# First loads in another order, keys and values of the second batch at later ticks, means of v in two column groups of TensorE

## The chip, the cores and the metric

The kernel runs on one core of one Trainium2 chip. The engines are TensorE (PE in the profile, its weight loads PEld), VectorE (DVE), ScalarE (ACT), GpSimd (POOL) and SyncE (SP), which here only issues loads and stores. The metric is the device time of one execution in microseconds; lower is better.

## The reference

Three layers follow each other: an attention with a window, a feed-forward layer with a softmax-like gate and a normalization, and a second feed-forward layer with ELU.

```python
# q, k, v: 2 batches, 8 heads, 768 positions, 64 channels
k_sum = k.reshape(B, H, nb, 32, D).max(axis=3)
v_sum = v.reshape(B, H, nb, 32, D).mean(axis=3)
scores_l = scale * q @ k.T            # kept where abs(i - j) < 16
scores_s = scale * q @ k_sum.T + log(32)
a = softmax(concat(scores_l, scores_s))
x = a @ concat(v, v_sum)              # 1536 tokens x 512
h = x @ w_in                          # 512 x 1024
solu = h * softmax(h)
ln = (solu - mean) / sqrt(var + 1e-6) * g_ln
x2 = ln @ w_out                       # 1024 x 512
h2 = x2 @ w_in2                       # 512 x 2048
out = elu(h2) @ w_out2                # 2048 x 512
```

The matrices w_in, w_out, w_in2 and w_out2 arrive as 64-bit floats (the `words` of the launch are their halves).

## The kernel before, in words

**Attention.** A unit n is 64 positions of one batch, all eight heads; there are 24, twelve per batch. `attn_s(n)` copies the 96 keys of its window beside the 24 block maxima into one of three buffers `kw` on POOL, multiplies on PE (`s_ps`, with `q_bd[n]`, a load of 256 KB), adds the mask and takes the maximum on DVE, takes the exponential on ACT, the reciprocal on DVE, and scales the four head pairs on POOL (`sm`). `attn_p(n)` transposes on PE (`p_ps`) and copies on ACT (`pT`). `attn_x(n)` multiplies with the values (`x_ps`; `vw`, three buffers, with 96 rows of v loaded by `load_v` and 24 rows of block means copied from `vsum` on POOL), and splits the result into a hi part (ACT) and a lo part (DVE), `xT`. Each value product writes 64 of the 128 output partitions: the even head of a pair the lower half, the odd head the upper.

**Sums over blocks.** `load_k(b)` loads the keys of a batch, four loads of 400 KB; `sum_k(b)` takes the block maxima with four reductions on DVE. `sum_v(b)` loads v in six tiles of 256 KB into the buffer `y[1]` (`rows[1]`) and forms the means with six matmuls of 512 columns with the matrix `avg`, which moves along so that the 24 sums of all six tiles add up in rows 96 to 119 of one PSUM tile, `vs_ps`; one ACT copy takes them to `vsum`.

**Conversions.** `convert` loads 512 KB of 64-bit words into a part of `y[0]` or `y[1]` (named y_65 and y_66 in the program) and makes 32-bit floats of them: ACT (line 113), POOL (114), DVE (115, 116, 117), then the hi part on ACT (120) and the lo part on DVE (95). For w_in there are eight such chunks, six buffers in turn (`early`); the last three of them lie in `y[1]`, where the v tiles lie too. Eight chunks of w_out follow (line 119 on POOL multiplies with g_ln). `more()` does the next one.

**Feed-forward.** A token tile j is 128 tokens. `mm_in(j, n)` is one half of h, twelve matmuls of 512 columns (`h`); after the second half `ffn1_ln(j)` begins with the row maximum on DVE (line 233). `mm_out` and the second layer follow.

**Order.** SP issues its loads in the order in which the code stands (a manual schedule), and waits at each for its buffer. The order on the other engines comes from a scheduler that works on the whole program. First comes a start written out by hand, and then a loop over 24 ticks, of which each does one half of h and the steps of attention units t+6 (scores), t+4 (transposes) and t+3 (values).

Of the kernel before, what the change touches and what calls it, by code (L numbers as in the profile page):

```python
# [14 lines left out]
AF = mybir.ActivationFunctionType  # L15
# [4 lines left out]
B, H, S, D = 2, 8, 768, 64  # L20
BLOCK, WINDOW = 32, 16
NB = S // BLOCK
TQ = 64
NT = S // TQ
WIN = 96
KW = WIN + NB
# [23 lines left out]
def tile_kernel(ctx: ExitStack, tc: tile.TileContext, qd, kT, v, w_in, w_out, g_ln, w_in2, w_out2,  # L50
                ident_d, mask_d, avg_d, out):
    nc = tc.nc
# [7 lines left out]
    ident = com.tile([128, 128], F32, name="ident")  # L60
# [20 lines left out]
    gT = p_ln.tile([128, KF1], F32, name="gT")  # L81
# [5 lines left out]
    avg = p_at.tile([128, 128 + NB], F32, name="avg", bufs=1)  # L87
    nc.gpsimd.memset(negh, -0.5)

    def copy_pool(out_, in_):  # L90
        nc.gpsimd.tensor_scalar(out_, in_, 1.0, 0.0, op0=ALU.mult, op1=ALU.add)


    def lo_of(out_, x, hi):
        nc.vector.tensor_tensor(out_, x, hi.bitcast(F32), op=ALU.subtract)  # L95
# [38 lines left out]
    k_sb, q_bd, xT, live, ksum, vsum = {}, {}, {}, {}, {}, {}  # L134

    def load_k(b):
        k_sb[b] = p_k.tile([128, NP, S + 2 * PAD], F32, tag="k", name="k_sb", bufs=2)
        for p in range(NP):
            nc.sync.dma_start(k_sb[b][:, p, :], kT[b, p])

    def sum_k(b):
        ksum[b] = p_at.tile([128, NP, NB], F32, name="ksum") if b else kws[0][:, :, WIN:KW]
        for p in range(NP):
            nc.vector.tensor_reduce(
                ksum[b][:, p, :], k_sb[b][:, p, PAD:PAD + S].rearrange("d (n j) -> d n j", j=BLOCK),
                axis=AX.X, op=ALU.max)


    def sum_v(b):
        pst = psb.tile([128, DM], F32, tag="b", name="vs_ps")  # L150
        for i in range(S // 128):
            vt = rows[1][i]
            nc.sync.dma_start(vt, v[b, PAD + i * 128:PAD + (i + 1) * 128, :])
            c0 = NB - i * 4
            nc.tensor.matmul(pst, lhsT=avg[:, c0:c0 + 128], rhs=vt, start=i == 0, stop=i == S // 128 - 1)
        vsum[b] = p_at.tile([128, DM], F32, tag="vsum", name="vsum", bufs=1)
        nc.scalar.activation(vsum[b][WIN:KW, :], pst[WIN:KW, :], AF.Copy)

    def load_q(n):
        q_bd[n] = p_at.tile([128, NP, 2 * TQ], F32, tag="q", name="q_bd", bufs=4)  # L160
        nc.sync.dma_start(q_bd[n], qd[n])

    def load_v(n):
        b, t = divmod(n, NT)
        nc.sync.dma_start(vws[n % NBUF][0:WIN, :], v[b, t * TQ:t * TQ + WIN, :])

    def attn_s(n):
        b, t = divmod(n, NT)
        j, half = divmod(n, 2)
        kw = kws[n % NBUF]  # L170
        if n not in q_bd:
            load_q(n)
        if t < NBUF and n:
            copy_pool(kw[:, :, WIN:KW], ksum[b])
        copy_pool(kw[:, :, 0:WIN], k_sb[b][:, :, t * TQ:t * TQ + WIN])
        sps = psb.tile([128, NP, 128], F32, tag="b", name="s_ps")
        for p in range(NP):
            nc.tensor.matmul(sps[:, p, 0:KW], lhsT=q_bd[n][:, p, :], rhs=kw[:, p, :], start=True, stop=True)  # L178
        sm = p_at.tile([128, NP, KW], F32, tag="sm", name="sm", bufs=NBUF)
        st = p_at.tile([128, 4, NP], F32, tag="st", name="st", bufs=NBUF)  # L180
        nm, ss, ri = (st[:, i, :] for i in range(3))
        mi = 1 if t == 0 else (2 if t == NT - 1 else 0)
        for p in range(NP):
            nc.vector.tensor_tensor_reduce(sm[:, p, :], sps[:, p, 0:KW], mask[:, mi, :], -scale, 3.0e38,
                                           op0=ALU.add, op1=ALU.min, accum_out=nm[:, p:p + 1])
        for p in range(NP):
            nc.scalar.activation(sm[:, p, :], sm[:, p, :], AF.Exp, bias=nm[:, p:p + 1], scale=-1.0,
                                 accum_out=ss[:, p:p + 1])
        nc.vector.tensor_scalar(ri, ss, 1e-9, None, op0=ALU.add)
        nc.vector.reciprocal(ri, ri)  # L190
        for p in range(NP):
            nc.gpsimd.tensor_scalar(sm[:, p, :], sm[:, p, :], ri[:, p:p + 1], 1.0, op0=ALU.mult, op1=ALU.mult)  # L192
        live[n] = sm
    def attn_p(n):
        pps = psb.tile([128, NP, 128], F32, tag="b", name="p_ps")
        for p in range(NP):
            nc.tensor.transpose(pps[:KW, p, :], live[n][:, p, :], ident)
        pT = p_at.tile([128, NP, 128], F32, tag="pT", name="pT")
        nc.scalar.activation(pT[:KW], pps[:KW], AF.Copy)
        live[n] = pT  # L200

    def attn_x(n):
        b, t = divmod(n, NT)
        j, half = divmod(n, 2)
        if t < NBUF:
            copy_pool(vws[n % NBUF][WIN:KW, :], vsum[b][WIN:KW, :])
        pT, vw = live.pop(n), vws[n % NBUF]
        if not half:
            xT[j] = [p_at.tile([128, NP, 128], F32R, tag=f"x{i}", name="xT", bufs=3) for i in range(2)]
        xps = psb.tile([128, NP, 128], F32, tag="b", name="x_ps")[:, :, :TQ]  # L210
        for p in range(NP):
            for hh in range(2):
                ds = slice(hh * D, (hh + 1) * D)
                nc.tensor.matmul(xps[ds, p, :], lhsT=vw[:KW, p * 128 + hh * D:p * 128 + (hh + 1) * D],  # L214
                                 rhs=pT[:KW, p, hh * TQ:(hh + 1) * TQ], start=True, stop=True)
        xh, xl = (a[:, :, half * TQ:(half + 1) * TQ] for a in xT[j])
        nc.scalar.activation(xh, xps, AF.Copy)
        lo_of(xl, xps, xh)
# [58 lines left out]
    def load_w3():  # L277
        f = len(w3)
        if f < 2:
            t = p_k.tile([128, 2, KD, 128], F32R, name=f"w3_{f}")  # L280
        elif f < 14:
            if f in (2, 5):
                state["k"] = p_k.tile([128, 3, 2, KD, 128], F32R, name=f"w3_{f}", tag="k", bufs=2)
            elif f in (8, 11):
                state["k"] = p_w3.tile([128, 3, 2, KD, 128], F32R, name=f"w3_{f}", tag=f"lnT{f // 11}")
            t = state["k"][:, (f - 2) % 3]
        else:
            t = p_w3.tile([128, 2, KD, 128], F32R, name=f"w3_{f}")
        w3.append((t[:, 0], t[:, 1]))
        convert(bits(), w_in2[:, f * 128:(f + 1) * 128].bitcast(I32).rearrange("(k p) f -> p k f", p=128),  # L290
                t[:, 0], t[:, 1])
# [33 lines left out]
    def more(n=1):  # L325
        for _ in range(n):
            if conv:
                conv.pop(0)()

    def mm_in(j, n):  # L330
        for k in range(KD):
            ffn1_in(j, n, k)
        if n == 1:
            ffn1_ln(j)
# [10 lines left out]
    loads = tc.manual_schedule(engines={mybir.EngineType.SP})  # L345
    loads.__enter__()
    load_k(0)
    load_q(1)
    load_v(0)
    nc.sync.dma_start(mask, mask_d)  # L350
    sum_k(0)
    nc.sync.dma_start(ident, ident_d)
    load_q(0)
    more()
    nc.sync.dma_start(avg, avg_d)
    attn_s(0)
    more()
    attn_s(1)
    sum_v(0)
    more(2)  # L360
    attn_p(0)
    attn_p(1)
    attn_s(2)
    attn_x(0)
    load_v(1)
    attn_x(1)
    nc.sync.dma_start(gT, g_ln)
    attn_s(3)
    load_v(2)
    attn_p(2)  # L370
    attn_s(5)
    attn_x(2)
    more(3)
    attn_p(3)
    attn_s(4)
    load_v(3)
    more()

# [9 lines left out]
    NU = B * NT  # L390
    for t, (j, n) in enumerate(ticks):
        s_n, p_n, x_n = t + LEAD, t + LEAD - 2, t + LEAD - 3
        if t == 0:
            sum_v(1)
        elif t == 1:
            load_k(1)
        elif t == 3:
            sum_k(1)
        if x_n < NU and t:
            load_v(x_n)  # L400
        if s_n < NU:
            for u in (s_n + 1, s_n):
                if u < NU and u not in q_bd:
                    load_q(u)
            attn_s(s_n)
        mm_in(j, n)
        if p_n < NU:
            attn_p(p_n)
        for f, *args in after[t]:
            f(*args)  # L410
        if x_n < NU:
            attn_x(x_n)
        more(converts.get(t, 0))
        if t in (13, 15):
            load_w3()
        if x_n == NU - 1:
            p_at.release()
            p_w3 = ctx.enter_context(tc.tile_pool(name="p_w3", bufs=1, side="left", reuse_waits="tile"))
            lnT_last = [p_w3.tile([128, KF1, TB], F32R, tag=f"lnT{c}", name="lnT") for c in range(2)]
# [134 lines left out]
```

## Time and profile before

| | |
|---|---|
| median of 3 runs | 507.53 us (506.18 to 510.06) |
| profiled execution | 510.05 us, span 508.3 us |
| PE busy | 482.9 us, 95% of the span |
| DVE busy | 292.2 us, 57% |
| ACT busy | 269.9 us, 53% |
| POOL busy | 136.3 us, 27% |
| loaded from memory | 42.93 MB |

The span is the time from the first to the last instruction; the execution's own time is 1.75 us longer. The shares are averages over stages that differ: the attention and the conversions lie in the first 200 us, the second layer in the last 300. Times below are counted from the span's start.

### The profile page before, as it was taken

The page shows a single profiled execution, that of the slowest core. Times are in us where ns is not written, and L with a number is a line of the kernel's source. Part 1 is how long each engine was busy: PE and PEld are TensorE (multiplying, and loading weights), DVE is VectorE, ACT ScalarE, POOL GpSimd, SP SyncE. Part 2 cuts the span into 40 slices and gives each one's busy share as a digit, 9 for nine tenths or more (in the row PEclk, how much of TensorE's full clock was granted, in tenths as well). Part 3 has the DMA queues.
Part 4 walks back from the last instruction along what each step waited for, and adds up shares of the span by engine and source line. Part 5 has one row for each costly group of instructions (what it writes and reads, how often), then busy time and mean ns, then how long its engine had stood idle before and what let it go on. Part 6 is the DMA issues. An engine that isn't in the chain of part 4 may idle for free.

```text
span 508.3 us, 7746 instructions
## 1 busy us (share of the span) xinstructions
PE 482.9 (95%) x2808; PEld 425.3 (84%) x2808; DVE 292.2 (57%) x714; ACT 269.9 (53%) x634; POOL 136.3 (27%) x216
## 2 busy tenths in 40 slices
PE   0888999899999999999999999999999999999997
PEld 0564877688888898999889999999998999999895
DVE  2688899697557126899999982222542323232331
ACT  1674898685657235766777763424452424242441
POOL 1877579589323111322132600000000000000000
PEclk9989999999999999999999999999999999999999
DMA  8967662261301010556455500000030000000003
GB/s 289 334 216 278 204 217 92 77 212 59 114 17 33 17 41 1 166 171 202 142 190 165 166 0 2 1 1 0 1 124 1 0 1 0 1 0 1 1 1 125
DMA packets 24567, 46.58 MB, mean 92 GB/s; under 512 B 2256, under 2 KB 11088, under 8 KB 24528
## 3 DMA queue, kind: packets, MB, share of 16 engines
q1 hardware_dynamic: 24528, 46.08, 28.1%
q8 instruction: 22, 0.36, 0.3%
q14 instruction: 17, 0.14, 0.1%
HBM read 42.93 MB, written 3.15 MB: 91 GB/s over the span
## 4 chain that ended last, share of the span: by engine, by line
PE 72%; DVE 12%; DMA 8%; ACT 3%; issue 2%; SPq 1%; POOL 1%; ACTq 0%; DVEq 0%
PE h L98 11%; PE h L100 11%; PE h L99 11%; PE o_ps L100 9%; PE o_ps L98 9%; PE o_ps L99 9%; DMA y<-in_w_out 4%; PE s_ps L178 3%; DVE conv L116 3%; DMA q_bd<-in_qd 3%; PE y_ps L98 2%; PE y_ps L100 2%; DVE conv L117 2%; PE y_ps L99 2%; PE x_ps L214 2%
## 5 line engine op out<-in xcount | busy, mean ns | idle before, releaser
L449 DVE SCALAR_TENSOR_TENSOR m<-m,h 128x384 f32<-128x384 f32 x64 | 35.2, 551 | 100.6 <-ACT m L448 100.6
L98 PE MATMUL h<-y_hl,w 128*128 128x384 f32 x256 | 86.2, 337 | 0.0
L100 PE MATMUL h<-y_hl,w 128*128 128x384 f32 x256 | 86.2, 337 | 0.0
L99 PE MATMUL h<-y_hl,w 128*128 128x384 f32 x256 | 86.2, 337 | 0.0
L447 ACT ACTIVATE m<-h 128x384 f32<-128x384 f32 x64 | 31.2, 487 | 84.4 <-PE h L100 84.3
L98 PE MATMUL o_ps<-w,g_hl 128*128 128x512 f32 x192 | 75.5, 393 | 0.1
L99 PE MATMUL o_ps<-w,g_hl 128*128 128x512 f32 x192 | 75.3, 392 | 0.0
L100 PE MATMUL o_ps<-w,g_hl 128*128 128x512 f32 x192 | 74.0, 392 | 0.0
L114 POOL TENSOR_SCALAR conv<-conv 128x512 f32<-128x512 f32 x48 | 38.2, 798 | 70.8 <-ACT conv L113 69.6
L192 POOL TENSOR_SCALAR sm<-sm,st 128x120 f32<-128x120 f32 x96 | 47.9, 518 | 23.1 <-DVE st L190 20.7
L95 DVE TENSOR_TENSOR g_hl<-m,g_hl 128x384 fp32r<-128x384 f32 x64 | 37.1, 580 | 27.3 <-ACT g_hl L450 27.2
L450 ACT ACTIVATE g_hl<-m 128x384 fp32r<-128x384 f32 x64 | 33.5, 524 | 33.9 <-DVE m L449 33.9
L99 PEld LDWEIGHTS h<-y_hl,w 128*128 128x128 f32 x256 | 48.0, 188 | 1.6
L98 PEld LDWEIGHTS h<-y_hl,w 128*128 128x128 f32 x256 | 48.0, 187 | 1.6
L100 PEld LDWEIGHTS h<-y_hl,w 128*128 128x128 f32 x256 | 48.0, 187 | 0.1
L178 PE MATMUL s_ps<-kw,q_bd 128*128 128x120 f32 x192 | 29.6, 301 | 15.5 <-DMA q_bd<-in_qd 14.0
L113 ACT ACTIVATE conv<-y 128x512 f32<-128x512 f32 x40 | 27.2, 679 | 32.1 <-DMA y<-in_w_in 11.4
L98 PE MATMUL y_ps<-lnT,w_out 128*128 128x384 f32 x128 | 43.8, 342 | 0.0
L99 PE MATMUL y_ps<-lnT,w_out 128*128 128x384 f32 x128 | 43.1, 337 | 0.0
L100 PE MATMUL y_ps<-lnT,w_out 128*128 128x384 f32 x128 | 42.8, 337 | 0.0
L100 PEld LDWEIGHTS o_ps<-w,g_hl 128*128 128x128 f32 x192 | 36.0, 188 | 7.8
L98 PEld LDWEIGHTS o_ps<-w,g_hl 128*128 128x128 f32 x192 | 36.0, 188 | 7.0 <-ACT g_hl L450 0.5
(77 smaller groups left out, 924.6 us busy)
## 6 DMA issues: line engine op xcount, KB each, us to landing
y<-in_w_out SPq DMA_DIRECT2D x23, 512.0 KB, 3.8
y<-in_w_in SPq DMA_DIRECT2D x17, 512.0 KB, 5.5
q_bd<-in_qd SPq DMA_DIRECT2D x24, 256.0 KB, 4.9
vw<-in_v SPq DMA_DIRECT2D x24, 192.0 KB, 4.1
bits<-in_w_in SPq DMA_DIRECT2D x7, 512.0 KB, 3.7
k_sb<-in_kT SPq DMA_DIRECT2D x8, 400.0 KB, 5.7
y<-in_v SPq DMA_DIRECT2D x12, 256.0 KB, 4.4
out<-y SPq DMA_DIRECT2D x11, 256.0 KB, 2.3
```

What stands on the lines that cost most here:

```text
L95: nc.vector.tensor_tensor(out_, x, hi.bitcast(F32), op=ALU.subtract)
L98: nc.tensor.matmul(ps, lhsT=l[0][ls], rhs=r[0][rs], start=first, stop=False)
L99: nc.tensor.matmul(ps, lhsT=l[0][ls], rhs=r[1][rs], start=False, stop=False)
L100: nc.tensor.matmul(ps, lhsT=l[1][ls], rhs=r[0][rs], start=False, stop=last)
L113: nc.scalar.activation(x, high.bitcast(F32), AF.Abs)
L114: nc.gpsimd.tensor_scalar(x, x, F64_HUGE, F64_TINY, op0=ALU.min, op1=ALU.max)
L116: nc.vector.scalar_tensor_tensor(a, high, -0x40000000, a, op0=ALU.bitwise_and, op1=ALU.bitwise_or)
L178: nc.tensor.matmul(sps[:, p, 0:KW], lhsT=q_bd[n][:, p, :], rhs=kw[:, p, :], start=True, stop=True)
L192: nc.gpsimd.tensor_scalar(sm[:, p, :], sm[:, p, :], ri[:, p:p + 1], 1.0, op0=ALU.mult, op1=ALU.mult)
L447: nc.scalar.activation(m, h2, AF.Relu, scale=-1.0)
L449: nc.vector.scalar_tensor_tensor(m, m, -1.0, h2, op0=ALU.add, op1=ALU.max)
L450: nc.scalar.activation(gh, m, AF.Copy)
```

## The change

Three things change. The loads of the start come in another order: q of unit 0 and the mask directly behind the keys, then q of unit 1, `avg` and the v tiles, and the identity, the value windows and the chunks of w_in after them. `load_k(1)`, `sum_k(1)` and `sum_v(1)` stand at ticks 2, 5 and 7 in place of ticks 1, 3 and 0. And the means use matmuls with 64 output partitions: tiles 0 to 2 add up in the lower half of the PSUM tile, 3 to 5 in the upper, taken in the order 0, 3, 1, 4, 2, 5; two ACT copies bring them together.

```diff
     def sum_v(b):
         pst = psb.tile([128, DM], F32, tag="b", name="vs_ps")
-        for i in range(S // 128):
+        for i in (0, 3, 1, 4, 2, 5):
             vt = rows[1][i]
             nc.sync.dma_start(vt, v[b, PAD + i * 128:PAD + (i + 1) * 128, :])
-            c0 = NB - i * 4
-            nc.tensor.matmul(pst, lhsT=avg[:, c0:c0 + 128], rhs=vt, start=i == 0, stop=i == S // 128 - 1)
+            g, c0 = i // 3, KW - 32 - i * 4
+            nc.tensor.matmul(pst[g * 64:(g + 1) * 64, :], lhsT=avg[:, c0:c0 + 64], rhs=vt,
+                             start=i % 3 == 0, stop=i % 3 == 2)
         vsum[b] = p_at.tile([128, DM], F32, tag="vsum", name="vsum", bufs=1)
         nc.scalar.activation(vsum[b][WIN:KW, :], pst[WIN:KW, :], AF.Copy)
+        nc.scalar.activation(vsum[b][WIN:WIN + NB // 2, :], pst[32:32 + NB // 2, :], AF.Copy)
...
     load_k(0)
-    load_q(1)
-    load_v(0)
+    load_q(0)
     nc.sync.dma_start(mask, mask_d)
     sum_k(0)
-    nc.sync.dma_start(ident, ident_d)
-    load_q(0)
-    more()
+    attn_s(0)
+    load_q(1)
     nc.sync.dma_start(avg, avg_d)
-    attn_s(0)
-    more()
     attn_s(1)
     sum_v(0)
-    more(2)
+    nc.sync.dma_start(ident, ident_d)
+    load_v(0)
+    more()
+    load_v(1)
+    more()
     attn_p(0)
     attn_p(1)
...
-        if t == 0:
+        if t == 2:
+            load_k(1)
+        elif t == 5:
+            sum_k(1)
+        elif t == 7:
             sum_v(1)
-        elif t == 1:
-            load_k(1)
-        elif t == 3:
-            sum_k(1)
```

The rest of the start (units 2 to 5, the six further chunks, g_ln) is rearranged in the same way. The order on the engines shows it. In these rows k_sb, q_bd, vw, mask, ident and avg are the tiles named above, y_65 the buffers of chunks 0, 1, 2, 6 and 7 of w_in, and y_66 those of chunks 3 to 5 and of the v tiles. Line numbers of the new kernel are up to 9 higher.

SP, the first loads of the program, before:

```order
L139 DMA k_sb<-in_kT 128x800 x4
L161 DMA q_bd<-in_qd 128x512
L165 DMA vw_101<-in_v 96x512
L350 DMA mask<-in_mask 128x360
L352 DMA ident<-in_ident 128x128
L161 DMA q_bd<-in_qd 128x512
L107 DMA y_65<-in_w_in 128x1024
L355 DMA avg<-in_avg 128x152
L107 DMA y_65<-in_w_in 128x1024
L153 DMA y_66<-in_v 128x512 x6
```

SP, the same place, now:

```order
L139 DMA k_sb<-in_kT 128x800 x4
L164 DMA q_bd<-in_qd 128x512
L352 DMA mask<-in_mask 128x360
L164 DMA q_bd<-in_qd 128x512
L356 DMA avg<-in_avg 128x152
L154 DMA y_66<-in_v 128x512 x6
L359 DMA ident<-in_ident 128x128
L168 DMA vw_101<-in_v 96x512
L107 DMA y_65<-in_w_in 128x1024
L168 DMA vw_102<-in_v 96x512
```

The first q was unit 1's and the second unit 0's; now unit 0 is first. The six v tiles moved ahead of all chunks of w_in.

POOL, from the key copy of unit 3 (into kw_98) to the copies of the means into the value windows, before; sm is the scaling of the scores, conv a step of a conversion:

```order
L91 TENSOR_SCALAR kw_98<-k_sb 128x4x96
L114 TENSOR_SCALAR conv<-conv 128x512
L91 TENSOR_SCALAR kw_99<-k_sb 128x4x96
L114 TENSOR_SCALAR conv<-conv 128x512
L192 TENSOR_SCALAR sm<-sm,st 128x120 x8
L114 TENSOR_SCALAR conv<-conv 128x512
L91 TENSOR_SCALAR vw_101<-vsum 24x512
L91 TENSOR_SCALAR vw_102<-vsum 24x512
L91 TENSOR_SCALAR vw_103<-vsum 24x512
```

POOL, the same place, now:

```order
L91 TENSOR_SCALAR kw_98<-k_sb 128x4x96
L91 TENSOR_SCALAR kw_99<-k_sb 128x4x96
L195 TENSOR_SCALAR sm<-sm,st 128x120 x8
L91 TENSOR_SCALAR vw_101<-vsum 24x512
L91 TENSOR_SCALAR vw_102<-vsum 24x512
L91 TENSOR_SCALAR vw_103<-vsum 24x512
L114 TENSOR_SCALAR conv<-conv 128x512 x2
```

The three conversion steps that stood ahead of the copies of the means stand behind them.

PE, where the means of the second batch stood among the matmuls of the first token tile, before:

```order
L178 MATMUL s_ps<-kw_99,q_bd 128x120 x4
L155 MATMUL vs_ps<-y_66,avg 128x512 x2
L98 MATMUL h<-w_in_82,xT 128x512
L197 MATMUL p_ps<-ident,sm 120x128 x2
L99 MATMUL h<-w_in_83,xT 128x512
L100 MATMUL h<-w_in_82,xT 128x512
L197 MATMUL p_ps<-ident,sm 120x128
L155 MATMUL vs_ps<-y_66,avg 128x512 x2
```

PE, where they stand now, between the value product of unit 9 and the matmuls of the fifth token tile (t_ps are the transposes of the normalized rows):

```order
L256 MATMUL t_ps<-ident,ln 128x128 x8
L217 MATMUL x_ps<-pT,vw_101 64x64 x8
L156 MATMUL vs_ps<-y_66,avg 64x512 x6
L98 MATMUL h<-w_in_82,xT 128x512
L99 MATMUL h<-w_in_83,xT 128x512
L181 MATMUL s_ps<-kw_99,q_bd 128x120 x4
```

The six matmuls moved behind those of four token tiles, and follow each other without another between them.

## Rows read from the trace of the kernel before

**Rows 1.** Busy time by stretch: us, then each engine's busy us, clock, DMA share, GB/s:

```profile
0.00:16.25 16.25, 4.60 (x19) 4.12 (x20) 5.55 (x21) 4.16 (x12) 3.88 (x13) 1.00 0.91 310
16.25:25.00 8.75, 6.57 (x24) 3.13 (x23) 6.86 (x16) 5.60 (x15) 8.33 (x12) 1.00 0.99 310
25.00:28.80 3.80, 3.80 (x44) 3.49 (x43) 2.12 (x11) 2.23 (x11) 2.58 (x4) 0.55 1.02 393
28.80:64.80 36.00, 31.76 (x222) 22.62 (x221) 31.00 (x108) 24.42 (x79) 24.99 (x44) 1.00 0.65 209
64.80:120.00 55.20, 51.68 (x386) 41.94 (x385) 48.98 (x170) 45.11 (x137) 43.72 (x73) 1.00 0.47 151
120.00:508.00 388.00, 384.49 (x2125) 349.99 (x2123) 197.67 (x394) 188.40 (x386) 52.78 (x73) 1.00 0.18 55
```

**Rows 2.** Waits of PE, 10 to 60 us: us in total, times, longest:

```profile
PE s_ps L178 <- DMA q_bd<-in_qd: 14.0, 3, 11.6
```

**Rows 3.** Timeline of SP's queue: start us, us, what is issued:

```profile
33.00 8.69 SPq L153 DMA_DIRECT2D y<-in_v  x6
```

**Rows 4.** The chain of work that ended last, 0 to 60 us: start us, us:

```profile
5.19 6.32 DMA q_bd<-in_qd
...
17.52 6.82 DMA q_bd<-in_qd
```

**Rows 5.** Timeline of PE, several stretches: start us, us, what, count:

```profile
11.65 3.68 PE L178 MATMUL s_ps<-kw,q_bd 128*128 128x120 f32 x16 [11.65 <-DMA q_bd<-in_qd]
15.16 4.53 PE L155 MATMUL vs_ps<-y,avg 128*128 128x512 f32 x10
...
25.60 1.98 PE L214 MATMUL x_ps<-pT,vw 120*64 120x64 f32 x32
...
38.24 1.89 PE L155 MATMUL vs_ps<-y,avg 128*128 128x512 f32 x4
...
63.90 0.50 PE L98 MATMUL h<-w_in,xT 128*128 128x512 f32 x1
...
96.87 0.69 PE L214 MATMUL x_ps<-pT,vw 120*64 120x64 f32 x16
97.48 1.15 PE L178 MATMUL s_ps<-kw,q_bd 128*128 128x120 f32 x8
```

**Rows 6.** Groups of DVE, 0 to 120 us: count, busy us, mean ns of one:

```profile
L116 DVE SCALAR_TENSOR_TENSOR conv<-y,conv 128x512 int32<-128x512 int32 x16 | 13.3, 831 | 0.2
L117 DVE SCALAR_TENSOR_TENSOR conv<-y,conv 128x512 int32<-128x512 int32 x16 | 11.7, 729 | 0.1
L115 DVE TENSOR_SCALAR conv<-conv 128x512 int32<-128x512 int32 x16 | 8.3, 521 | 1.0 <-POOL conv L114 1.0
...
L95 DVE TENSOR_TENSOR w_in<-conv,w_in 128x512 fp32r<-128x512 f32 x8 | 5.6, 695 | 1.4 <-ACT w_in L120 1.3
```

**Rows 7.** Timeline of DVE, three places: start us, us, what:

```profile
8.82 0.95 DVE L144 TENSOR_REDUCE kw<-k_sb 128x24 f32<-128x768 f32 x1 [0.50 <-DMA k_sb<-in_kT]
...
16.25 0.42 DVE L115 TENSOR_SCALAR conv<-conv 128x512 int32<-128x512 int32 x1
...
64.81 1.21 DVE L233 TENSOR_REDUCE st<-h 128x1 f32<-128x1024 f32 x1
```

**Rows 8.** Timeline of POOL, two stretches: start us, us, what, count:

```profile
17.25 5.62 POOL L192 TENSOR_SCALAR sm<-sm,st 128x120 f32<-128x120 f32 x8
...
23.65 2.57 POOL L91 TENSOR_SCALAR vw<-vsum 24x512 f32<-24x512 f32 x3
...
56.03 2.77 POOL L192 TENSOR_SCALAR sm<-sm,st 128x120 f32<-128x120 f32 x8 [3.57 <-DVE st L190]
```

**Rows 9.** Timeline of ACT, 12 to 27 us:

```profile
12.85 0.67 ACT L113 ACTIVATE conv<-y 128x512 f32<-128x512 f32 x1 [10.85 <-DMA y<-in_w_in]
...
21.86 0.59 ACT L157 ACTIVATE vsum<-vs_ps 24x512 f32<-24x512 f32 x1
```

**Rows 10.** Timeline of ACT around 93 us:

```profile
93.10 0.68 ACT L113 ACTIVATE conv<-y 128x512 f32<-128x512 f32 x1 [2.62 <-DMA y<-in_w_out]
```

More of the change, by code (lines that the diff above doesn't have):

```diff
@@ L347, in tile_kernel @@
     load_k(0)
-    load_q(1)
-    load_v(0)
+    load_q(0)
     nc.sync.dma_start(mask, mask_d)
     sum_k(0)
-    nc.sync.dma_start(ident, ident_d)
-    load_q(0)
-    more()
+    attn_s(0)
+    load_q(1)
     nc.sync.dma_start(avg, avg_d)
-    attn_s(0)
-    more()
     attn_s(1)
     sum_v(0)
-    more(2)
+    nc.sync.dma_start(ident, ident_d)
[3 more added lines that the diff above has]
+    more()
     attn_p(0)
     attn_p(1)
+    attn_x(0)
+    attn_x(1)
+    load_q(2)
+    more()
+    load_q(3)
+    load_v(2)
     attn_s(2)
[L364 to L367, printed above, removed]
+    more()
     attn_s(3)
-    load_v(2)
     attn_p(2)
-    attn_s(5)
     attn_x(2)
-    more(3)
-    attn_p(3)
-    attn_s(4)
     load_v(3)
     more()
+    attn_p(3)
+    load_q(4)
+    more()
+    attn_s(4)
+    load_q(5)
+    more(2)
+    attn_s(5)
+    nc.sync.dma_start(gT, g_ln)
     ticks = [(0, 0), (1, 0), (0, 1), (1, 1)] + [(j, n) for j in range(2, NJ) for n in range(2)]
```

## The prediction, made blind

> **What bounds the kernel now.** I read the table of busy time by stretch first [rows 1]. From 120 us on PE is busy 384 of 388 us: whatever happens there is fixed work, and a kernel that arrives at that point earlier by x ends earlier by x. Before 120 us PE is busy 98.4 us and idles for 21.6, of which 11.65 lie ahead of its first matmul [rows 5]. So the change, which touches only the first 100 us, can gain part of those 21.6 us and what it takes off PE's work. Who leads in that phase? From 28.8 to 64.8 VectorE (DVE) is busy 31.0 of 36 us, from 64.8 to 120 it is 49.0 of 55.2, ahead of ScalarE (ACT) with 45.1 and GpSimd (POOL) with 43.7. No engine alone is the bound there: work goes in a chain from engine to engine, and DVE has the least room, because each of the 16 weight conversions of this phase costs it four operations of 0.83, 0.73, 0.52 and 0.70 us, 2.8 in all (some 2.5 where their ends overlap) [rows 6]. Then I read what PE waits for up to 60 us [rows 2]: 14.0 us for three loads of q. Last, the load queue (SP): the first q that is needed is the ninth load and lands at 5.19 + 6.32 = 11.51 us, the third lands at 24.34 [rows 4]; and from 33.0 to 41.7 SP stands at the v loads of the second batch, because each writes a buffer that a conversion of w_in still reads [rows 3]; the next q and all keys of the second batch queue behind.
>
> **First scores.** Now q of tile 0 is the fifth load; 692 KB fewer lie ahead of it, 2.3 us at 310 GB/s [rows 1]. It then lands at about 9.2, and the maxima of the keys, which end at 8.82 + 0.95 = 9.77 [rows 7], are last. The first score matmul goes from 11.65 to about 9.9: **1.8 us**.
>
> **First part of the attention.** The means began at 15.16, when the first v tile was there, with 3,904 KB loaded through it; in the new order 3,904 KB go through the last v tile. So all six tiles are there at about 15, and the means end near 16, where the first ten of the twelve old records ended at 19.69 [rows 5]. The scaling on POOL started 5.6 us after the first scores (17.25 to 11.65) [rows 5, 8]; 0.5 of that was a conversion in its way, so it starts near 15.0. Eight scalings took 5.62 beside DVE's conversions, and 2.77 alone [rows 8]. DVE has almost nothing else then, so I take 2.8: done at 17.8. The second copy of the means on ACT (0.59, as the first [rows 9]) fits before that. Then come three copies of the means into the value windows, 2.57, the first done near 18.9. The first value product moves from 25.60 to about 19: **6.6 us earlier** for this step alone.
>
> **What that costs: the conversions.** The first w_in chunk has 4,672 KB through it instead of 3,060; its first ACT step began at 12.85 [rows 9], and 1.65 MB at 310 GB/s is 5.3 us, so near 18. POOL takes its step of the conversion only behind the eight scalings and three copies (17.8 + 2.6 = 20.5), and DVE starts at about **21.2 instead of 16.25** [rows 7]. Before that, DVE has done 4 maxima (3.8), 8 score operations (1.7), four small ones (0.6) and two lo parts (0.7): 6.8 us, so it was idle for 14.4. This is the price of loading in order of need: the engine with the least room starts its longest work 5 us later.
>
> **Sum on DVE to the second row maximum of the feed-forward**, which began at 64.81 [rows 7]. Before: busy 5.55 + 6.86 + 2.12 + 31.00 = 45.5 [rows 1], idle 19.3. In the new order DVE has one more first step and one more second step of a conversion ahead of that point (0.52 + 0.83) and two small operations fewer (about 0.5): 46.4. Idle: 14.4 to the first conversion, and after it what I find by following the order engine by engine: 0.7 for the hi part of the fourth chunk, 1.0 and 0.5 for the exponentials and the value product of units 7 and 4, 0.6 for the scores of unit 8; 2.8, and I take 3.3. Together 46.4 + 14.4 + 3.3 = 64.1: **0.7 us earlier**. On PE the third token tile's first matmul, in the same walk, moves from 63.9 [rows 5] to 62: **1.9 us**.
>
> **Means side by side.** Twelve records at 0.44 us (ten in 4.53 with the last one's tail [rows 5]) are 5.25 us per batch. If the two groups run fully beside each other it is 2.6. The trace has the case: the value products already go to two column groups, and 16 records of 64 columns take 0.61 us (96.87 to 97.48) [rows 5]. At the means' 0.86 ns a column they would take 0.88 one behind the other; so the factor lies between 0.69 (as measured with the switch in and out) and 0.5, and the saving between 1.6 and 2.6 a batch. I take 2.4, as the 0.69 holds a fixed cost that a long matmul hardly feels. But where is it worth anything? The first block waits for v and ends early whatever PE does. The second leaves 38 to 46 us, where PE waits for DVE anyway, and comes at tick 7 (some 80 us), where PE has 3.5 us of idle time in 55 [rows 1] and DVE leads: its 2.6 are mostly covered there. What lies behind it on PE is the score of unit 13, six ticks ahead of its use. Without that cover it costs 2.6. So I count nothing for the sizes and keep them for the bounds. The Trainium skill (TensorEngine Tiling (Array Packing), Key Properties) says that changing the tiling mode drains the engine, which speaks against this edit. The trace shows the switch twice around each value product, 0.61 against half of 0.88: at most 0.17 for both. By the rule the four new switches would add about 0.3 us.
>
> **Later loads.** The keys of the second batch no longer wait behind v: SP reaches them near 35 us instead of after 41.69 [rows 3], although they stand later in the program. v of the second batch now writes buffers whose last reader is done 40 us earlier, so SP does not stop; behind it in SP stand the q and v of units 10 to 14, which wait 3 us at most. The one extra ACT copy there (0.59) is in a stretch where ACT is busy 82%; between 0 and 0.6.
>
> **Sum.** Between 0.7 (by DVE) and 1.9 (by PE) are gained by 65 us, and nothing clear in either direction from there to 120: I take **2 us**. The profiled execution took 510.05 us, with 508.3 of span; it is the slowest of those shown, 2.5 above the median, and has ACT standing 2.62 us, until 93.1, for a w_out load [rows 10], about that much. So 510.05 - 2 = 508 if the stall comes again, and 507.53 - 2 = **505.5 us** against the median, which I forecast.
>
> **Rival 1, PE leads.** If the chain lets PE profit from its own two savings, 1.8 at the start and 2 x 2.6 of means, the time is 507.5 - 7.0 = 500.5. For it: PE's order then holds no means among the feed-forward matmuls of 38 to 46 us, and the q waits of [rows 2] vanish. Against it: DVE's 86% and more in 28.8 to 120. It decides where DVE waits under 1 us in 21 to 65. Chance 0.2.
>
> **Rival 2, slower: the late conversions.** DVE from 16.25 to 64.8 was idle 8.6 of 48.6 us [rows 1], for hops from engine to engine. If it loses as much again after 21.2, it is 46.4 + 14.4 + 8.6 = 69.4, 4.6 later: 512. And PE has little between 16 and 33 us now; in 25.0 to 28.8 its granted clock read 0.55 [rows 1], that is 1.2 for most of the stretch in place of 2.4 GHz, after a stretch of 8.75 us with 24 records in it. If that falls on the 24 matmuls of 0.23 us before 62 us that DVE holds back until then, up to 5.5 more: 517. It decides at 3.5 us of idle time beyond my 3.3. Chance 0.17, of which 0.11 over 1%.
>
> **Rival 3, the groups do not run beside each other**, or a drain eats it: 2.6 more at 80 us, partly covered: 506 to 508. Chance 0.08.
>
> **How the numbers follow.** The forecast (503 to 508) has 0.55. One per cent is 5 us, about what a measurement can tell. Faster by more needs under 502.5: most of rival 1, 0.17, and the low edge of the forecast, 0.04: 0.21. Slower by more needs over 512.6: 0.11 of rival 2. Within: 0.68. The range goes from rival 1's end, 500.5, to 511, just short of rival 2's.
>
> **What would show it.** First scores near 9.9; the first value product near 19 to 20; DVE's first conversion at 21; the six means in about 2.7 us at tick 7, in pairs; no SP stop at v; second row maximum at 63 to 65. I am wrong if conversions start at 17 to 18 (gain of 5 and more), if DVE has gaps of over 6 us between 21 and 65, or if the granted clock is at half for more than 4 us after 30 us.

## The result, and the profile of the changed kernel

The changed kernel takes 509.46 us (median of 20 runs, 507.88 to 510.66), the kernel before, timed beside it, 506.36 us (20 runs, 504.56 to 510.06). The ratio is 1.0055, 95% interval 1.0042 to 1.0067: 0.55% or 2.8 us slower (the medians lie 3.1 apart), where 2 us less were forecast. The time lies in the range, on the wrong side. The profiled execution took 508.92 us with a span of 507.2. The profiled execution that the prediction read (510.05, span 508.3) was one of the longest of its kernel, so a second one of before stands beside it here: 506.34 us, span 504.5 (the first run of the next section). Against that one the loss is made early: the last matmul with w_in (`h`) starts at 199.88 us in place of 197.32, and what follows takes as long in either, 307.3 and 307.2 us.

Busy time by stretch of the changed kernel, the stretches of [rows 1], and two longer ones (us; busy us of PE, PE's weight loads, DVE, ACT, POOL; granted clock; DMA share; GB/s):

```profile
0.00:16.25 16.25, 7.06 (x28) 4.54 (x28) 6.22 (x24) 4.53 (x17) 5.19 (x18) 1.00 0.90 304
16.25:25.00 8.75, 4.94 (x58) 3.88 (x56) 4.06 (x14) 6.58 (x18) 6.20 (x11) 1.00 1.04 315
25.00:28.80 3.80, 2.01 (x3) 0.79 (x3) 3.80 (x17) 3.36 (x11) 0.63 (x2) 0.51 1.02 386
28.80:64.80 36.00, 30.22 (x199) 24.09 (x200) 30.25 (x101) 22.58 (x74) 24.42 (x40) 0.77 0.53 171
64.80:120.00 55.20, 53.83 (x402) 43.86 (x401) 49.44 (x174) 46.21 (x135) 45.83 (x78) 1.00 0.55 178
...
0.00:50.00 50.00, 29.44 (x171) 21.08 (x172) 33.53 (x111) 26.50 (x82) 26.09 (x48) 0.82 0.80 265
50.00:120.00 70.00, 68.63 (x517) 56.07 (x516) 60.24 (x215) 56.76 (x169) 56.18 (x99) 0.98 0.53 169
```

The same two longer stretches in the second profile of the kernel before:

```profile
0.00:50.00 50.00, 32.82 (x192) 21.69 (x193) 34.28 (x102) 25.26 (x75) 31.15 (x52) 1.00 0.86 290
50.00:120.00 70.00, 68.27 (x512) 55.74 (x512) 62.41 (x227) 56.54 (x175) 55.73 (x96) 1.00 0.48 152
```

The rows from 0 to 50 and from 50 to 120 us are the key. In either kernel PE idles up to 50 us, for 17 us before and 21 now (11.59 and 9.19 of them ahead of its first matmul), and from 50 to 120 it is busy 98% of the time. The split at 28.8 and 64.8 in [rows 1] hid that border: the stretch to 64.8 mixes a part in which PE waits with one in which it sets the pace. That suggests a rule, which the experiments test: what PE can do in its waits before 50 us is free, as far as the waits reach, and what stands behind them is paid.

PE's timeline in the changed kernel, several places (start us, us, what, count, idle time before and what ended it), which answers to [rows 5]:

```profile
9.19 3.74 PE L181 MATMUL s_ps<-kw,q_bd 128*128 128x120 f32 x16 [9.19 <-POOL kw L91]
12.86 3.74 PE L156 MATMUL vs_ps<-y,avg 128*64 128x512 f32 x12
...
19.33 1.39 PE L217 MATMUL x_ps<-pT,vw 120*64 120x64 f32 x32 [1.71 <-POOL vw L91]
...
44.86 0.51 PE L98 MATMUL h<-w_in,xT 128*128 128x512 f32 x1 [3.21 <-ACT w_in L120]
47.14 0.47 PE L200 MATMUL p_ps<-ident,sm 128*120 128x128 f32 x1 [1.78 <-POOL sm L195]
...
65.72 0.48 PE L98 MATMUL h<-w_in,xT 128*128 128x512 f32 x1
...
85.00 0.69 PE L217 MATMUL x_ps<-pT,vw 120*64 120x64 f32 x16 [1.09 <-issue]
85.59 2.79 PE L156 MATMUL vs_ps<-y,avg 128*64 128x512 f32 x12
```

DVE of the changed kernel at three places (answers to [rows 7]), and the load queue at two (answers to [rows 3]):

```profile
20.48 0.42 DVE L95 TENSOR_TENSOR xT<-x_ps,xT 128x256 fp32r<-128x256 f32 x1 [5.15 <-ACT xT L220]
21.67 0.56 DVE L115 TENSOR_SCALAR conv<-conv 128x512 int32<-128x512 int32 x1
...
64.79 1.21 DVE L236 TENSOR_REDUCE st<-h 128x1 f32<-128x1024 f32 x1
```

```profile
38.19 1.85 SPq L139 DMA_DIRECT2D k_sb<-in_kT  x4
...
67.11 3.03 SPq L154 DMA_DIRECT2D y<-in_v  x6
```

The front of the program came out to within a microsecond: scores at 9.19, value products at 19.33, first conversion at 21.67, second row maximum at 64.79, no stop of the queue at v, the six matmuls of the means at tick 7 (twelve records, two to a matmul) in 2.79 us. What did not come is PE's lead at the third token tile: 65.72 against 63.90 in [rows 5], and 62.78 in the second profile of before, although PE no longer has the means of the second batch ahead of it. From there the two kernels can be followed tile by tile. The fourth begins at 75.98 us, 1.6 later than in the second profile of before; the fifth, which stands behind the moved means, at 88.32, 4.0 later (84.35).

And what PE waits for in the changed kernel, 20 to 72 us (us in total, times, longest), which answers to [rows 2]:

```profile
PE h L98 <- ACT w_in L120: 5.1, 3, 3.2
PE p_ps L200 <- POOL sm L195: 2.0, 2, 1.8
PE h L99 <- DVE w_in L95: 1.4, 2, 1.0
PE s_ps L181 <- DMA q_bd<-in_qd: 1.1, 1, 1.1
```

These are waits for converted chunks of w_in above all, 6.5 us; the second profile of before has 0.6 us of them, and 0.9 for q (of the 14.0 for q in [rows 2], 11.6 lie ahead of the first matmul). There PE did its means between the matmuls of the chunks, from 36 to 44 us, and started its third token tile at 62.78:

```profile
36.31 1.89 PE L155 MATMUL vs_ps<-y,avg 128*128 128x512 f32 x4
...
39.06 1.88 PE L155 MATMUL vs_ps<-y,avg 128*128 128x512 f32 x4
...
41.60 1.98 PE L155 MATMUL vs_ps<-y,avg 128*128 128x512 f32 x4
...
62.78 0.50 PE L98 MATMUL h<-w_in,xT 128*128 128x512 f32 x1
```

### The profile page after: what moved, and what is told of

The parts are those of the page before. It is cut to its first block, busy times and chain, and to the rows that moved or that the text cites. A ratio compares the mean times of both kernels' runs of the same rounds, so it can differ in the third digit from the quotient of the medians.

```text
span 507.2 us, 7728 instructions
## 1 busy us (share of the span) xinstructions
PE 481.5 (95%) x2808; PEld 426.7 (84%) x2808; DVE 290.8 (57%) x714; ACT 271.8 (54%) x636; POOL 133.0 (26%) x216
## 4 chain that ended last, share of the span: by engine, by line
PE 91%; DVE 4%; POOL 2%; DMA 1%; issue 1%; ACT 1%; SPq 0%; POOLq 0%
PE h L98 13%; PE h L99 13%; PE h L100 13%; PE o_ps L98 9%; PE o_ps L100 9%; PE o_ps L99 9%; PE s_ps L181 4%; PE y_ps L100 4%; PE y_ps L99 4%; PE y_ps L98 4%; PE x_ps L217 3%; PE p_ps L200 2%; PE t_ps L256 2%; PE vs_ps L156 1%; DMA k_sb<-in_kT 1%; POOL sm L195 1%
## 5 line engine op out<-in xcount | busy, mean ns | idle before, releaser
L195 POOL TENSOR_SCALAR sm<-sm,st 128x120 f32<-128x120 f32 x96 | 45.3, 490 | 22.2 <-DVE st L193 20.9
L190 ACT ACTIVATE sm<-sm,st 128x120 f32<-128x120 f32 x96 | 36.7, 385 | 18.7 <-DVE st L187 18.6
L98 PE MATMUL h<-w_in,xT 128*128 128x512 f32 x96 | 40.9, 426 | 5.1 <-ACT w_in L120 5.1
```

Source lines behind the costliest of these rows:

```text
L98: nc.tensor.matmul(ps, lhsT=l[0][ls], rhs=r[0][rs], start=first, stop=False)
```

## The experiments

All ratios are to the kernel before, timed beside each run on the same chip (its medians there were 506.6 to 507.3 us). 0.1% is 0.5 us. By the intervals, a difference between two rows is sure to some 1 to 2 us, so the smaller ones below (0.8 to 1.4 us) are at the edge of what can be told. The three runs with no_second_means in their name leave out work: they use the means of the first batch for both.

| run | ratio | 95% interval |
|---|---|---|
| only_loads | 1.0048 | 1.0025 to 1.0071 |
| only_ticks | 1.0104 | 1.0073 to 1.0134 |
| only_groups | 1.0072 | 1.0045 to 1.0100 |
| loads_and_ticks | 1.0108 | 1.0088 to 1.0127 |
| loads_and_groups | 1.0115 | 1.0099 to 1.0132 |
| no_second_means | 1.0010 | 0.9993 to 1.0027 |
| w_in_first | 1.0028 | 1.0010 to 1.0046 |
| w_in_first_no_second_means | 0.9994 | 0.9976 to 1.0012 |
| old_no_second_means | 1.0069 | 1.0041 to 1.0097 |
| second_means_at_tick_3 | 1.0029 | 1.0015 to 1.0044 |
| q0_and_w_in_first | 1.0019 | 0.9999 to 1.0040 |
| means_early | 0.9994 | 0.9980 to 1.0008 |
| means_early_w_in_first | **0.9925** | 0.9901 to 0.9949 |
| v_tiles_in_new_order | 1.0005 | 0.9989 to 1.0021 |
| own_buffers_for_v | 0.9986 | 0.9971 to 1.0000 |
| early_without_groups | 1.0008 | 0.9985 to 1.0030 |
| own_buffers_and_groups | 0.9975 | 0.9958 to 0.9992 |

**The kernel before, profiled again** (no edit):

> The kernel before, unchanged, profiled once more. The first profile of it took 510.05 us against a median of 506.4, so I expect a span 2 to 4 us shorter, and from where: without ACT's 2.6 us wait for the w_out load near 90 us (so DVE's gap of 3.08 us near 95 gone) and perhaps with chunk 3 of w_in and q of unit 2 landing 1 to 2 us earlier. If the gap is there again, the profile is typical and the medians differ by something later than 100 us.

506.34 us, and the granted clock is 1.00 throughout; the 0.55 of [rows 1] at 25 to 28.8 us doesn't belong to every execution.

**The three parts, each alone.** only_loads takes the new order of the first loads and leaves the rest as before; only_ticks moves only keys and v of the second batch to ticks 2, 5 and 7; only_groups takes only the new means. Each is a piece of the diff ahead of the prediction (only_loads with the whole start).

> The kernel before with the new order of the first loads alone. Theory 'late conversions and slow clock' (DVE starts converting 5 us later, PE has little to do from 16 to 33 us, its granted clock halves and makes the matmuls of the first token tile slow): slower by 2 to 5 us, ratio 1.004 to 1.010. Theory 'the ticks' (the means of the second batch cost PE and ACT at 70 to 85 us): faster by 1 to 3 us.

> The kernel before with keys and v of the second batch at the later ticks alone. Late conversions: the same or faster by up to 2 us, since SP no longer stops at the v loads. Theory 'the ticks': slower by 2 to 5 us, and if so the 5.25 us of means stand in a stretch where PE has no idle time.

> The kernel before with the means in two column groups alone. Late conversions and the ticks both expect 0 to 2.6 us faster. Theory 'the groups cost more than they give' (second ACT copy, drains, matmuls not side by side): slower by 0.5 to 2 us. In the trace, six matmuls should take 2.6 us when they stand together, and 5.2 if they do not overlap.

Each part is slower by itself. The ticks alone cost 1.04% or 5.3 us, and PE's timeline has the means at the new place with about that length:

```profile
86.03 5.42 PE L155 MATMUL vs_ps<-y,avg 128*128 128x512 f32 x12
```

The two need not be one and the same, since in this run PE also works at half clock from 41.56 to 55.22 us (see Rival 2 below). The groups alone should have saved or cost little. Busy time of that run, and PE around 66 us, show a second price:

```profile
60.00:70.00 10.00, 6.92 (x57) 5.54 (x57) 9.64 (x36) 10.00 (x36) 4.54 (x10) 0.75 0.40 130
```

```profile
66.05 0.47 PE L199 MATMUL p_ps<-ident,sm 128*120 128x128 f32 x1 [2.34 <-POOL sm L194]
...
68.95 0.63 PE L98 MATMUL h<-w_in,xT 128*128 128x512 f32 x1
69.37 0.63 PE L99 MATMUL h<-w_in,xT 128*128 128x512 f32 x1
...
71.93 0.40 PE L99 MATMUL h<-w_in,xT 128*128 128x512 f32 x1
```

PE waited 2.34 us in the part where it sets the pace, and the ten matmuls from 67.50 on then started some 0.43 us apart instead of 0.23, at the half clock: 2 us more. Together that is more than the 3.6 us of the ratio. The wait ends with POOL's scaling, but from 60 to 70 us POOL is busy for 4.5 us and ACT for all 10, so which engine was late isn't settled. The groups don't cost this by themselves (own_buffers_and_groups, below).

**Two parts together.**

> The changed kernel, but with the old means of v (no column groups, one copy). Theory means at tick 7 (the means of the second batch cost PE nothing among the waits of 36 to 44 us, and their full length at 86 us): 5.4 us of means there in place of 2.8, so 2.6 more than the changed kernel, 511.5 to 512.5, ratio to before 1.010 to 1.012. Theory late conversions and slow clock (the loss is made between 20 and 60 us): the same start as the changed kernel, so at most 1 us from it, 508.5 to 510.5. Theory order luck (any edit makes the order of the other engines worse by 2 to 5 us): anything from 508 to 512, without relation to the length of the means.

> The changed kernel, but keys and v of the second batch at the old ticks. Theory means at tick 7: the means lie among PE's waits again, so 2 to 3 us faster than the changed kernel, 506 to 507.5. Theory late conversions and slow clock: the start is that of the changed kernel, 509 to 511, as with the loads alone (509.57). Theory order luck: 508 to 512.

Loads and ticks came as the theory of the means at tick 7 says: 1.0108.

```profile
87.73 5.42 PE L155 MATMUL vs_ps<-y,avg 128*128 128x512 f32 x12
```

This is the cleanest pair of the series. But for the means, full-width here and in column groups there, the changed kernel has the same program; it has 2.79 us of them at this place, 2.63 less, and is 2.7 us faster (1.0055). So, to about 1 us, the shorter means of the first batch gave nothing, and those at tick 7 are paid in full.

Loads and groups did not come as the theory says. The load queue of that run, and below it that of only_loads:

```profile
33.69 10.59 SPq L153 DMA_DIRECT2D y<-in_v  x6
...
45.27 2.27 SPq L139 DMA_DIRECT2D k_sb<-in_kT  x4
...
33.13 10.70 SPq L153 DMA_DIRECT2D y<-in_v  x6
```

The conversions run later, so the buffers that v needs come free later; the stop at v is 10.59 us instead of 8.69 [rows 3], and the keys follow at 45 us. That can't be what makes 1.0115: only_loads has the same stop, its keys follow at 44.83 us, and it stands at 1.0048. What does is open. The later ticks are no gain of their own. With the groups they are worth 3 us (1.0115 to 1.0055), with the old means they cost 3 (1.0048 to 1.0108).

**Taking the suspected costs out, one and both.**

```diff
 def sum_v(b):
+    if b:                       # no_second_means
+        for i in (0, 3, 1, 4, 2, 5):
+            nc.sync.dma_start(rows[1][i], v[b, PAD + i * 128:PAD + (i + 1) * 128, :])
+        vsum[1] = vsum[0]
+        return
...
     attn_s(1)
+    more(2)                     # w_in_first
     sum_v(0)
     nc.sync.dma_start(ident, ident_d)
     load_v(0)
-    more()
     load_v(1)
-    more()
```

> The changed kernel without the twelve matmul records and two copies that make the means of v of the second batch; its v tiles are still loaded, and the means of the first batch are used in their place. Up to the fourth token tile every engine has the order of the changed kernel. Theory means at tick 7: the 2.8 us come off in full, 506.3 to 507 (2.4 to 3.1 below the changed kernel), so without them the changed kernel is level with the kernel before, which has them. Theory late conversions and slow clock: PE waits for DVE there, at most 1 us comes off, 508.4 to 509.5. Theory order luck: not in proportion, 507 to 511.

> The changed kernel with the first two chunks of w_in loaded ahead of the six v tiles, so that DVE can convert from about 13 to 16 us on, as in the kernel before; means and value products then come some 4 us later. Theory late conversions and slow clock: the loss goes, 504.5 to 507. Theory means at tick 7: within 1 us of the changed kernel, 508.5 to 510.5. Theory order luck: 508 to 512.

> Both repairs of the changed kernel at once: two chunks of w_in ahead of v, and no means of the second batch. If the two are separate causes, what each gave adds up (2.3 and 1.35 of ratio to before): 3.6 below the changed kernel, ratio to before 0.996 to 0.9995. If they are one cause seen twice, no more than the larger, ratio 1.000 to 1.002.

Without the second means 1.0055 becomes 1.0010: 2.3 us of their 2.79 were paid. With two chunks of w_in ahead of v it becomes 1.0028, 1.4 us, between the two theories. Both edits give 0.9994, which is what two causes would give; the interval, up to 1.0012, reaches into the range of a single one. The pair below with all work kept (means_early) settles that.

**The same means taken out of the kernel before** (the edit of no_second_means), and **put at tick 3 of the changed kernel**:

```diff
-    elif t == 7:
+    elif t == 3:                # second_means_at_tick_3
         sum_v(1)
```

> The kernel before without the means of v of the second batch (its v tiles are still loaded, the means of the first batch are used in their place). Theory free before 50 us, paid after (DVE sets the pace up to about 50 us, PE from there on): the 5.4 us of means lay among PE's waits of 36 to 44 us, so taking them out gains at most 1 us, 506.3 to 507.3. Rival, the means always cost what they take: 502 to 503.5. Order luck (the other engines' order is planned anew): 505 to 511 without relation to the means.

> The changed kernel with v and means of the second batch at tick 3 in place of 7; PE's order then has the means near 60 us. Theory free before 50 us, paid after: at 60 us PE leads just as at 86, so within 1 us of the changed kernel, ratio 1.004 to 1.008. Theory means at tick 7 (the place at 86 us, with its waits for the normalized rows, is what costs): 1.5 to 2.5 faster than the changed kernel, ratio 1.000 to 1.003.

Both missed. The first has 5.4 us less work on PE and is 3.5 us slower. Up to the third token tile it shows what was expected. Where the means had stood PE now waits for chunks of w_in, 4.0 us up to 50 us in place of 0.6, and the tile begins at 63.22 us, no earlier than with the means (62.78):

```profile
PE h L98 <- ACT w_in L120: 2.7, 2, 1.5
...
PE h L99 <- DVE w_in L95: 1.3, 2, 0.6
```

So most of the time that the means had taken became waiting (and, from 40.3 to 47.1 us, work at half clock): there they were close to free. The loss is made later, and the waits of PE from 75 to 100 us name a place:

```profile
PE x_ps L219 <- DVE lnT L95: 2.0, 1, 2.0
PE p_ps L202 <- DVE lnT L95: 1.1, 1, 1.1
```

The scheduler laid the engines' work in another order when the means were gone (sixteen transposes in a row ahead of the value product at 83.66 us, where the second profile of before has twice eight, with matmuls between), and PE stood 3.1 us for a product of DVE that cost 0.7 in the second profile of before. The second run, with the means at 58.92, gained 1.3 us, less than at 40 us (below) and more than expected. One difference is in the traces: the changed kernel has a stop of 1.09 us ahead of the value product at 85.00 (the row is above), no_second_means has it too, and this run doesn't. Whether that is why 59 is cheaper than 86 stays open.

**Earlier q and w_in in the kernel before.**

```diff
     load_k(0)
-    load_q(1)
-    load_v(0)
+    load_q(0)
     nc.sync.dma_start(mask, mask_d)
     sum_k(0)
+    more()
+    load_q(1)
+    load_v(0)
     nc.sync.dma_start(ident, ident_d)
-    load_q(0)
-    more()
     nc.sync.dma_start(avg, avg_d)
```

> The kernel before, with q of tile 0, the mask and one chunk of w_in as the first loads behind the keys, and q of tile 1, v and the identity after them; nothing else moved. Theory free before 50 us, paid after: what counts is when DVE has the first six chunks done; DVE starts its first conversion 2 to 4 us earlier, so 1 to 3 us faster than before, 504.5 to 506.5. Order luck: 507 to 511.

1.0019, no gain; the expectation missed. DVE's first conversion moved from 16.26 to 14.13 us, and that alone is worth nothing in the kernel before.

**The means where PE waits.** Until the first token tile comes through (its row maximum is at 59 us in the changed kernel), three of the five buffers of the normalized rows are unused. They take v of the second batch at tick 0, with nothing to wait for:

```diff
 def sum_v(b):
+    if b:
+        own = [p_ln.tile([128, F1], F32, tag="ln", name="own", bufs=5) for _ in range(3)]
...
-    vt = rows[1][i]
+    vt = own[i // 2][:, i % 2 * DM:(i % 2 + 1) * DM] if b else rows[1][i]
...
-    if t == 2:
+    if t == 0:
+        sum_v(1)
+    elif t == 2:
         load_k(1)
     elif t == 5:
         sum_k(1)
-    elif t == 7:
-        sum_v(1)
```

> The changed kernel with v of the second batch loaded at tick 0 into three buffers that are free until 55 us, so that its twelve means records stand near 40 us in PE's order, ahead of PE's 3.2 us wait for a chunk of w_in. Theory free before 50 us, paid after: the 2.3 us that leaving the means out gave come back in full, ratio to before 0.9995 to 1.0025, 2 to 3 us under the changed kernel, although all work is done. Order luck: no relation, 1.003 to 1.010.

> The same with two chunks of w_in loaded ahead of the v tiles of the first batch. Theory free before 50 us, paid after: both causes are undone with all work kept, so as fast as the kernel without the means, ratio 0.997 to 1.0005. Order luck: 1.003 to 1.010.

PE's timeline of means_early:

```profile
37.38 2.80 PE L157 MATMUL vs_ps<-own,avg 128*64 128x512 f32 x12
...
43.75 0.49 PE L98 MATMUL h<-w_in,xT 128*128 128x512 f32 x1 [1.79 <-ACT w_in L120]
```

The means are as long as at tick 7, but the wait behind them is 1.79 us instead of 3.21, and PE goes on at 43.75 instead of 44.86. The ratio is 0.9994: 3.1 us come back, with all work kept. PE's waits for w_in hardly shrink (6.2 us in all, as another of 1.60 ends at 50.20), but the half clock does (under Rival 2, below), so a part of the 3.1 can be the clock's. With w_in first as well it is 0.9925, **3.8 us faster than the kernel before** and 6.6 faster than the changed one. PE's waits of that run, 16 to 50 us, show the rest:

```profile
PE h L98 <- ACT w_in L120: 0.7, 1, 0.7
PE h L99 <- DVE w_in L95: 0.6, 1, 0.6
```

6.5 us of waits for w_in have become 1.3. Neither edit alone comes near this (1.0028 and 0.9994), so there are two causes, where the chunks of w_in are loaded and where the means stand.

**Order, buffers and groups by themselves.** The first run below has v's new tile order with the old means (`for i in (0, 3, 1, 4, 2, 5)`, nothing else); the second gives the kernel before the three buffers, at its own ticks; the third adds the groups to the second; the last takes the groups out of the fastest kernel.

> The kernel before with the six v tiles of a batch loaded and summed in the order 0, 3, 1, 4, 2, 5; no column groups, no other edit, the same work. If only work and waits count: ratio 0.999 to 1.002. If the order that is planned for the other engines counts, as for the column groups alone (1.0072): 1.003 to 1.009.

> The kernel before with v of the second batch in three buffers of its own, so that the load queue doesn't stop for some 8.7 us at 33 us, and keys and q behind it come earlier; means still near 40 us. Theory free before 50 us, paid after: the stop was no bound, within 1 us, ratio 0.998 to 1.002. Rival, the stop costs: 2 to 4 us faster, 0.992 to 0.996. Order luck: 1.003 to 1.009.

> The kernel before with v of the second batch in buffers of its own and the means as column groups; start and ticks as before. Theory free before 50 us, paid after: all means lie before 50 us, so within 1.5 us of own_buffers_for_v (0.9986), 0.9965 to 1.001. Rival, groups cost by themselves (as alone, 1.0072): 1.004 to 1.008.

> The kernel of means_early_w_in_first with the old means (six full-width matmuls a batch in order 0 to 5, one copy), all else as there. Theory free before 50 us, paid after: both means lie before 50 us, so the 2.6 us that the groups save in the second batch are worth little there, within 1.5 us of it, ratio to before 0.9925 to 0.9965. Rival, groups gain what they save wherever they stand: 2.5 us slower than it or more, 0.9975 to 1.000. Rival, groups cost by themselves: faster than it, 0.988 to 0.991.

The new order of the tiles does nothing, so it isn't true that any edit costs. The stop of the queue was no bound in the kernel before (0.9986), and the groups cost nothing when v does not wait for buffers (0.9975). The last run missed its expectation: without groups the fastest kernel falls back to 1.0008. Its PE timeline, with that of the fastest kernel below it, shows a part of why:

```profile
39.70 1.02 PE L157 MATMUL vs_ps<-own,avg 128*128 128x512 f32 x2
...
38.64 2.04 PE L157 MATMUL vs_ps<-own,avg 128*64 128x512 f32 x8
...
41.04 1.40 PE L157 MATMUL vs_ps<-own,avg 128*64 128x512 f32 x4
```

Without groups the six matmuls stand between 39.70 and 46.16 us and take 5.8 us in all, with groups 3.4; and PE has no wait for w_in left in the run without. As I read it, by then the means and not the chunks hold it up: a wait hides as much as it is long. That is 2.4 of the 4.2 us between the two runs; the rest is not settled.

## Why the prediction was wrong, step by step

- **First scores, First part of the attention, What that costs: the conversions.** Right: 9.19, 19.33 and 21.67 against 9.9, 19 and 21.2. The means of the first batch took 3.74 us in the trace, and no time was gained by that, as said.
- **Sum on DVE.** Right for DVE (64.79 for 64.1), wrong for PE: 62 was forecast for the third token tile, and it began at 65.72. The walk added up each engine's work and left out that PE would wait 6.5 us for w_in (0.6 in the second profile of before). What the late chunks cost depends on what else PE has to do: putting two ahead of v was worth 1.4 us in the changed kernel, 0.8 without the second means (1.0010 to 0.9994) and 3.5 with these means at 37 us (0.9994 to 0.9925). What the edit does to the clock is part of these figures: the twelve runs of w_in_first have a mean granted clock of 0.982 to 0.990, the twenty of the changed kernel 0.975 to 0.983. How much of the 1.4 us is waiting and how much is clock is not shown.
- **Means side by side.** The size was right: 2.79 us at tick 7, 5.42 without groups, so the groups do run beside each other, and Rival 3 falls. The Trainium skill's rule that a change of tiling mode drains the engine (TensorEngine Tiling (Array Packing), Key Properties) comes to 2.79 - 5.42 / 2 = 0.08 us here, less than the 0.3 estimated from [rows 5]. In means_early, where full-width matmuls stand on both sides, it is 0.09 (2.80). **The step that failed** is the cover: "PE has 3.5 us of idle time in 55 and DVE leads: its 2.6 are mostly covered there". PE leads from 50 us on. Of the 2.79 us, 2.3 come back when the means are left out, and the pair with loads_and_ticks has the full length paid. The 3.5 us were also read from one of the longest executions; the second profile of before has 1.7 in the same stretch. The prediction saw that the means leave a place where they cost nothing, and counted nothing for the place they went to. Both sentences side by side give the sign.
- **Later loads.** Right that the queue no longer stops and that this gains nothing by itself (own_buffers_for_v, in the kernel before).
- **Sum.** The 1.8 us of the first scores were worth nothing at 65 us, and the two costs together, measured in one run, are 3.1 us (1.0055 to 0.9994 in w_in_first_no_second_means), about the whole loss of 2.8. That the time still fell into the range is no merit of the sum.
- **Rival 2** had the right sign and a part of the cause. Its lateness of DVE did not come (second row maximum on time). Its half clock did: 0.51 at 25 to 28.8 us and 0.77 on average from there to 64.8 in the rows above, which is some 17 of these 36 us at 1.2 GHz, where the second profile of before has 1.00 throughout. The prediction named 4 us as the mark. What it cost is not measured. It came in two stretches, from 25.05 to 38.70 us and from 45.53 to 52.35. Behind the first PE still waits 3.21 us for a chunk, so that earlier matmuls could have meant a longer wait there. The second reaches behind the wait that ends at 47.14, the last before 84 us: 5.2 us of work at half clock, of which up to 2.6 are lost if PE alone sets the pace there (an estimate; DVE and POOL are busy for nearly all of that time too). From 47 to 55 us, in turn the changed kernel, means_early and only_ticks:

```profile
47.00:55.00 8.00, 7.86 (x45) 6.71 (x46) 6.39 (x22) 4.16 (x13) 8.00 (x15) 0.67 0.60 188
...
47.00:55.00 8.00, 6.40 (x45) 4.88 (x44) 7.19 (x22) 3.91 (x13) 4.62 (x10) 1.00 0.44 148
...
47.00:55.00 8.00, 6.50 (x36) 5.79 (x37) 4.51 (x17) 3.20 (x9) 4.97 (x9) 0.50 0.45 134
```

means_early does as many matmuls (45, not all the same ones) in 6.40 us as the changed kernel in 7.86. The pair of loads_and_ticks and the changed kernel is hardly touched by this, with a clock of 0.65 and 0.67 in the same stretch. The runs of one kernel don't settle the price. In the twelve of no_second_means the time goes with the mean granted clock (508.59 us and more at 0.975 and below, 506.28 and 507.01 at 0.986); in the twenty of the changed kernel it doesn't (a median of 508.36 in the five up to 0.976, of 509.71 in the six from 0.980 on). No run takes the half clock away and leaves the order as it is.

- **Rival 1** named the right leader, but let PE profit from both savings. PE got neither: its first scores came 2.4 us earlier, and it waited longer for w_in instead.

What stays open is the price of the half clock, and how much the plan of the scheduler adds: old_no_second_means lost 3.5 us with less work, loads_and_groups is 3 us slower than the changed kernel, and the places of such waits change from edit to edit. The 3.1 us that means_early returned, with the changed loads and groups kept, make chance an unlikely cause of the main loss; they don't exclude a part of it.

## What to carry to other kernels

Before a step is moved, find out for both places whether its engine waits there: cut the table of busy time where that engine's idle time ends, not at round or inherited borders, for one row that mixes both regimes makes a chain look like nobody's bound. Work that leaves a wait gains nothing, and work that arrives where the engine never idles costs up to its length, even if it was shortened on the way. Where a buffer forces the later place, look for another buffer first: here three idle ones took back a loss of 0.55%, and with two chunks of w_in loaded earlier there was a gain of 0.75%.

## What was unexpected of the hardware

- A matmul of one column group alone takes as long as a full-width one: in loads_and_groups each single one (two records) took 1.07 us, in early_without_groups a full-width one 1.02. Only two groups in direct succession share the time: twelve records in 2.79 us.

```profile
40.34 1.07 PE L155 MATMUL vs_ps<-y,avg 128*64 128x512 f32 x2
```

- A wait of PE can be paid twice: in only_groups 2.34 us of waiting (PE was busy 2.97 of the 5.09 us from 60.00 to 65.09), and then ten matmuls at the half clock for 2 us more.
- In four runs PE stood ahead of the value product behind the transposes at 83 to 87 us for nothing that the profile shows: 1.09 us in the changed kernel and in no_second_means, 2.21 in only_loads, 2.94 in own_buffers_and_groups. In the second profile of before it did not. I don't know why.

```profile
86.81 0.69 PE L214 MATMUL x_ps<-pT,vw 120*64 120x64 f32 x16 [2.21 <-issue]
```
